# One transposed tile per unit of queries or keys, with the bucket codes compared in PSUM

## The chip, the cores and the metric

The kernel runs on one core of a Trainium2 chip. The metric is the time of one execution on the device, in microseconds. Of the kernel before, three runs are known, with a median of 793.76 us (791.67 to 797.49), and one profiled execution.

## The reference

```python
def _attn_ref(q, k, v, proj):              # q, k, v: 2 x 8 heads x 768 x 64, proj: 64 x 6
    scale = 1.0 / np.sqrt(D)
    q_bits = (np.einsum('bhsd,dk->bhsk', q, proj) > 0).astype(np.int64)
    k_bits = (np.einsum('bhsd,dk->bhsk', k, proj) > 0).astype(np.int64)
    powers = 2 ** np.arange(n_bits)
    q_bucket = np.sum(q_bits * powers, axis=-1)
    k_bucket = np.sum(k_bits * powers, axis=-1)
    mask = q_bucket[:, :, :, None] == k_bucket[:, :, None, :]
    scores = scale * np.matmul(q, k.transpose(0, 1, 3, 2))
    scores = np.where(mask, scores, -1000000000.0)
    ...
    return np.matmul(attn, v)              # attn: softmax of scores

def reference(**kwargs):
    attn_out = _attn_ref(**attn_kwargs)
    x = attn_out.transpose(0, 2, 1, 3).reshape(B * S, H * D)     # 1536 tokens x 512
    x = _moe_ref(x=x, **moe_kwargs)        # x @ w_in, gelu by a sigmoid, @ w_out; 512 -> 2048 -> 512
    return _moe2_ref(x=x, **moe2_kwargs)   # top 2 of 8 experts, 512 -> 1024 -> 512 each
```

Attention is masked by hash buckets: a query sees only keys whose six sign bits under the projection equal its own. A dense layer and a layer of eight experts follow.

## The kernel before

The program has three parts that overlap: 96 attention steps, the dense layer in 6 chunks of 256 tokens, which starts when a chunk's heads are done, and the experts, which start when all tokens are routed. A step g is one block of 128 queries of one head: `qk` on TensorE (scores of 128 x 768 into a PSUM tile `s` of two banks, of which there are two), `rowmax` on VectorE (reads the scores, writes them to SBUF as `e` with their maximum), `expo` on ScalarE, `e_hi` on ScalarE and `e_lo` on VectorE (two float16 halves `er`), a DMA transposition of `er` into `et`, and `pv` on TensorE. In the first 16 steps TensorE transposes `e` instead (`e_turn`).

Queries and keys reach `qk` in units: 24 units of queries (two heads by 256 positions) and 16 units of keys (one head by 768 positions). A number is split into float16 parts, hi and lo. `qk` accumulates two products for a block: slot s=0 of `qt` and `kt` (128 rows: hi and lo parts stacked) and slot s=1 (76 rows: 64 of the hi part and 12 of the bucket code, 65504 or 0 in queries, -65504 or 0 in keys, so that each bit that differs pushes a score far down). For each unit the steps are:

- `load`, `stack_hi` (hi part on VectorE or GpSimd, the remainder on GpSimd), `stack_lo` (lo part on ScalarE), and a DMA transposition of stack `sa` into slot 0 of `qt` or `kt` (L170)
- `buckets`: per block of 128 positions two matmuls with the transposed block as weights and the projection as moving operand (L187, L188), which give 12 columns in the free columns 768 and up of an `s` tile; ScalarE copies them out to `pc` (L192)
- `one_hot`: VectorE compares the two halves of `pc` (L198, two instructions) and writes 0 or 1 into columns 64 to 75 of a second stack `sb`, whose first 64 columns hold the hi part and whose last 52 GpSimd has cleared (L140)
- `stack_end`: ScalarE scales the codes (L205), and a second DMA transposition brings `sb` into slot 1 (L206)

`stack_hi` also writes the hi part a second time, scaled by 1/32 (L150 on ScalarE or L152 on VectorE), since the products of both stacks have to add up in one scale.

All DMAs but the indirect ones are issued from SP's queue, in order. The order of the work comes from numbers in `PARAM`: a unit starts at a step of its own (`KA`, `QA`), `buckets` follow `BK` steps later, `one_hot` `OH` steps later. Up to step 99 a scheduler then sets the order on each engine; from step 100 on it is the order of the code.

Of the kernel before, what the change touches and what calls it, by code (L numbers as in the profile page):

```python
# [8 lines left out]
F32 = mybir.dt.float32  # L9
# [22 lines left out]
NT = S // 128  # L32
# [32 lines left out]

@with_exitstack
def fused(ctx: ExitStack, tc: tile.TileContext, q, k, v, proj, w_in, w_out, w_gate, w_noise, noise,
# [20 lines left out]
    pr = {nm: consts.tile([128, 3, NBITS], F16, name=f"p{nm}") for nm in "qk"}  # L88

    def proj_parts():  # L90
        p32 = rt.tile([128, NBITS], F32, name="p32", tag="zc", bufs=1)
        nc.sync.dma_start(p32[:64], proj)
        nc.sync.dma_start(p32[64:], proj)

# [33 lines left out]

    def stack_hi(nm, b, u):
        x = raw[nm, b, u]  # L130
        nh, n = (2, CT) if nm == "q" else (1, NT)
        if nm == "q":
            sa = att.tile([128, nh, n, 128], F16, name="qsa", bufs=1)
            sb = att.tile([128, nh, n, 128], F16, name="qsb", bufs=2)
        else:

            ks = moe.tile([128, 2, n, 128], F16, name="ks", tag="wraw" if b else "gt", bufs=PARAM["NW"] if b else 4)
            sa, sb = ks[:, 0:1], ks[:, 1:2]
        rows[nm, b, u] = sa, sb
# [7 lines left out]
        yield  # L147
        m, o = PARAM["SC"](nm, b), sa[:, :, :, h0:h0 + 64].rearrange(FL)
        if m == "A":
            nc.scalar.activation(o, hi, AF.Copy, scale=1.0 / SH)  # L150
        else:
            (nc.gpsimd if m == "P" else nc.vector).tensor_scalar(o, hi, 1.0 / SH, 0.0, op0=OP.mult, op1=OP.add)  # L152

    def stack_lo(nm, b, u):
        x = raw.pop((nm, b, u))
        sa, sb = rows[nm, b, u]
        hp, i = u
        h0 = 64 if nm == "q" else 0
        nc.scalar.activation(sa[:, :, :, h0:h0 + 64].rearrange(FL), x.rearrange(FL), AF.Copy, scale=SH)
        if nm == "q":  # L160
            xt = att.tile([128, 2, 2, CT, 128], F16, name="qt", bufs=3)
            qts[b, hp, i] = xt
        elif i == 0:
            xt = att.tile([128, 2, 2, NT, 128], F16, name="kt", bufs=4)
            kts[b, hp] = xt
# [3 lines left out]
        rows[nm, b, u] = sb, dst
        nc.sync.dma_start_transpose(dst[:, 0].rearrange("p h c t -> p (h c) t"), sa.rearrange("p h c d -> p (h c d)"))  # L170

    def buckets(nm, b, u):
        sb, xt = rows[nm, b, u]
        nh, n = (2, CT) if nm == "q" else (1, NT)
        w0 = nh * n * 2 * NBITS
# [3 lines left out]
        a0 = s.get("end", S)
        s["end"] = a0 + w0  # L180
        assert s["end"] <= 1024
        pb = s["ps"][:, a0:a0 + w0].rearrange("p (m k) -> p m k", k=2 * NBITS)
        w = pr[nm].rearrange("p a b -> p (a b)")
# [10 lines left out]
    def one_hot(nm, b, u):  # L194
        pc = bks.pop((nm, b, u))
# [711 lines left out]
    def start(g, f, *a):  # L907
        early.setdefault(g, []).append((f, a))
# [343 lines left out]
```

## Time and profile before

| | |
|---|---|
| median of 3 runs | 793.76 us (791.67 to 797.49) |
| profiled execution | 794.73 us, span 793.0 us |
| TensorE matmul | 703.5 us busy, 89% of the span |
| VectorE, ScalarE, GpSimd | 63%, 58%, 34% of the span |
| DMA queue of SP | 125.04 MB, 68.6% of the time of 16 DMA engines |

The span is what lies between the first and the last instruction of the profiled execution; its own time is 1.7 us longer. Shares of the span are means over stretches with different limits, so the stretches are read one by one. A busy time of TensorE counts instructions in flight and is not its peak rate.

### The profile page before, as it was taken

The page shows a single profiled execution, that of the slowest core. Times are in us where ns is not written, and L with a number is a line of the kernel's source. Part 1 is how long each engine was busy: PE and PEld are TensorE (multiplying, and loading weights), DVE is VectorE, ACT ScalarE, POOL GpSimd, SP SyncE. Part 2 cuts the span into 40 slices and gives each one's busy share as a digit, 9 for nine tenths or more (in the row PEclk, how much of TensorE's full clock was granted, in tenths as well). Part 3 has the DMA queues.
Part 4 walks back from the last instruction along what each step waited for, and adds up shares of the span by engine and source line. Part 5 has one row for each costly group of instructions (what it writes and reads, how often), then busy time and mean ns, then how long its engine had stood idle before and what let it go on. Part 6 is the DMA issues. An engine that isn't in the chain of part 4 may idle for free. (4 is left out here: it accounts for less than half of the span.)

```text
span 793.0 us, 14888 instructions
## 1 busy us (share of the span) xinstructions
PE 703.5 (89%) x5408; PEld 432.5 (55%) x5409; DVE 501.4 (63%) x1251; ACT 457.2 (58%) x974; POOL 265.8 (34%) x338
## 2 busy tenths in 40 slices
PE   1776778998988988889989999999999999999995
PEld 0444446646854665467448667466555545555452
DVE  7986889896876778568568815665744526345220
ACT  4688877766876687468658614445543534435220
POOL 7446455641453345025222223322031120302203
PEclk9976788999999999999999999999999999999998
DMA  8999589999999999995697581568978668484213
GB/s 218 234 277 260 164 193 187 274 260 215 179 200 185 174 187 212 187 186 98 101 182 138 102 286 27 132 245 205 277 120 250 179 133 251 64 266 85 28 17 44
DMA packets 266941, 139.19 MB, mean 176 GB/s; under 512 B 224176, under 2 KB 242672, under 8 KB 266864
## 3 DMA queue, kind: packets, MB, share of 16 engines
q1 hardware_dynamic: 260848, 125.04, 68.6%
q0 software_dynamic: 6016, 13.16, 9.4%
q8 instruction: 43, 0.70, 0.4%
q14 instruction: 34, 0.28, 0.1%
HBM read 61.48 MB, written 23.20 MB: 107 GB/s over the span
## 5 line engine op out<-in xcount | busy, mean ns | idle before, releaser
L468 PE MATMUL h<-xt,wi 128*128 128x256 f16 x1152 | 140.4, 278 | 9.5 <-ACT xt L394 5.6
L846 PE MATMUL ph<-xg,ew 128*128 128x400 f16 (+2 forms) x864 | 132.8, 314 | 1.0 <-DVE ht L857 1.0
L786 DVE SCALAR_TENSOR_TENSOR ew<-w,ew 128x1024 f16<-128x1024 f32 x64 | 77.7, 1225 | 86.3 <-ACT ew L785 86.3
L479 PE MATMUL px<-wo,gt 128*128 128x512 f16 x576 | 131.1, 380 | 0.0
L468 PEld LDWEIGHTS <-wi 128*128 128x128 f16 x1152 | 112.9, 100 | 31.3 <-issue 11.8
L877 PE MATMUL py<-ew,ht 128*128 128x512 f16 x576 | 126.0, 379 | 0.0
L251 PE MATMUL s<-kt,qt 128*128 128x512 f16 (+3 forms) x384 | 90.9, 359 | 36.6 <-DVE e L263 24.1
L894 POOL DMA_INDIRECT out_dram<-yo,ti x32 | 50.0, 1564 | 204.4 <-ACT yo L887 190.2
L846 PEld LDWEIGHTS <-ew 128*128 128x128 f16 x864 | 80.4, 98 | 51.0 <-issue 2.8
L320 DVE SCALAR_TENSOR_TENSOR er<-e,mx,er 128x768 f16<-128x768 f32 x68 | 72.1, 1063 | 43.7 <-ACT er L311 39.9
L877 PEld LDWEIGHTS <-ht 128*128 128x128 f16 x576 | 56.3, 98 | 66.8 <-issue 0.2
L263 DVE TENSOR_SCALAR_CACHE_REDUCE e<-s 128x768 f32<-128x768 f32 x96 | 90.6, 948 | 1.6 <-PE pt L290 0.5
L272 ACT ACTIVATE e<-e,mx 128x768 f32<-128x768 f32 x96 | 89.4, 931 | 1.7
L514 POOL TENSOR_TENSOR gt<-th,gt 128x512 f16<-128x512 f32 x48 | 57.3, 1194 | 98.0 <-ACT gt L512 97.9
L479 PEld LDWEIGHTS <-gt 128*128 128x128 f16 x576 | 55.0, 98 | 63.2 <-issue 1.3
L311 ACT ACTIVATE er<-e,mx 128x768 f16<-128x768 f32 x68 | 62.9, 930 | 33.0 <-DMA et<-er 31.3
L251 PEld LDWEIGHTS <-qt 76*128 76x128 f16 (+1 forms) x384 | 35.9, 103 | 67.5 <-issue 30.2
L887 ACT ACTIVATE yo<-py,wv 128x512 f32<-128x512 f32 x24 | 16.5, 687 | 93.7 <-PE py L877 57.1
L785 ACT ACTIVATE ew<-w 128x1024 f16<-128x1024 f32 x64 | 66.2, 1048 | 0.1
L856 ACT ACTIVATE ht<-ph 128x400 f16<-128x400 f32 (+2 forms) x72 | 33.4, 465 | 53.0 <-PE ph L846 52.5
L365 PE MATMUL pv<-et,vt 128*64 128x256 f16 x720 | 50.7, 283 | 8.7 <-DMA et<-er 8.5
L857 DVE SCALAR_TENSOR_TENSOR ht<-ph,ht 128x400 f16<-128x400 f32 (+2 forms) x72 | 37.5, 523 | 28.0 <-ACT ht L856 27.9
(230 smaller groups left out, 909.5 us busy)
## 6 DMA issues: line engine op xcount, KB each, us to landing
w<-in_moe_w_dram SPq DMA_DIRECT2D x64, 512.0 KB
wraw<-in_moe_w_in_dram SPq DMA_DIRECT2D x16, 512.0 KB
wraw<-in_moe_w_out_dram SPq DMA_DIRECT2D x16, 512.0 KB
slots<-blank SPq DMA_DIRECT2D x6, 1032.0 KB
v<-in_v_dram SPq DMA_DIRECT2D x24, 192.0 KB
out_dram<-zeros SPq DMA_DIRECT2D x13, 256.0 KB
k<-in_k_dram SPq DMA_DIRECT2D x16, 192.0 KB
q<-in_q_dram SPq DMA_DIRECT2D x24, 128.0 KB
```

The source lines that it names most:

```text
L251: nc.tensor.matmul(ps[:, n0 * 128:n1 * 128], qt[:kr, s, h, t, :], kt[:kr, s, h, n0:n1, :].rearrange("p c t -> p (c t)"), start=(s == 0), s ...
L263: nc.vector.tensor_scalar(e32, st[g]["ps"][:, :S], -FAR, -TOP, op0=OP.max, op1=OP.max, accum_out=mx[:, 0:1])
L272: nc.scalar.activation(e32, e32, AF.Exp, scale=0.125, bias=st[g]["mx"][:, 1:2], accum_out=sms[b, cc, hp][:, 2 * h + t:2 * h + t + 1] if g ...
L311: nc.scalar.activation(er[:, 0], st[g]["e"], AF.Copy, scale=r)
L320: nc.vector.scalar_tensor_tensor(er[:, 1], d["e"], d["mx"][:, 3:4], er[:, 0], op0=OP.mult, op1=OP.subtract)
L468: nc.tensor.matmul(ph[:, a, :], wi[ws][:, d, f0:f0 + 128], xt[:, d, xs, :], start=(d == 0 and ws == 0 and xs == 0), stop=(d == HP - 1 and ...
L479: nc.tensor.matmul(px, gts[ci, f // 2][:, gs, f % 2, t * 128:t * 128 + 128], wo[ws][:, f, :], start=(f == 0 and gs == 0 and ws == 0), stop ...
L514: eng.tensor_tensor(gt[:, 1], th, gt[:, 0], op=OP.subtract)
L785: nc.scalar.activation(hi, x, AF.Copy, scale=SW1 if j == 0 else SW2)
L786: nc.vector.scalar_tensor_tensor(lo, x, SW1 if j == 0 else SW2, hi, op0=OP.mult, op1=OP.subtract)
L846: nc.tensor.matmul(ph[:, :c1 - c0], w[:, ws, d * FE + f * 128:d * FE + f * 128 + 128], xg[e, p][:, xs * HP + d, :], start=(d == 0 and ws = ...
L877: nc.tensor.matmul(py, ht[:, f, hs, t * 128:t * 128 + 128], w[:, ws, f * DM:(f + 1) * DM], start=(i == 0), stop=(i == n - 1))
```

## The change

One stack per unit is transposed, not two. Its transposed slot 0 holds the hi and the lo part, and slot 1 takes its first 64 rows from slot 0 by a copy within SBUF (`second`: ScalarE for queries, 64 x 512, and GpSimd for keys, 64 x 768). `buckets` now has the projection (12 columns) as weights and the transposed blocks as moving operand, two blocks or 256 positions at a time, so that codes come out with codes on partitions: 2 groups of 12 partitions for a unit of queries, 3 for a unit of keys, each in a stretch of 32 partitions of its own, three accumulating matmuls per group, in the same free columns of an `s` tile. `codes` compares them where they are, in PSUM, with a threshold per partition, and writes 65504 or -65504 or 0 straight into rows 64 to 75 of slot 1 (12 x 256 per instruction, two instructions for a unit of queries, three for one of keys). The copy to `pc`, `one_hot`, `stack_end`, the scaled second hi part and the clearing of `sb` go away. `BK` goes from 3 to 2. The scale of the scores becomes 32 times as large, which `expo` takes back. Per run the DMA transpositions of queries and keys go from 80 to 40.

```diff
+PARAM.update(NH=lambda nm, b, hp: 2 if nm == "q" else 1, KC=lambda nm, b: "A" if nm == "q" else "D", EM=0, Q3=2, X3=4, QT=3)
+PARAM.update(KC=lambda nm,b:"A" if nm=="q" else "P")
+PARAM.update(BK=2,OH=3)
...
-        nc.gpsimd.memset(sb[:, :, :, KB:].rearrange(FL), 0.0)
-        h0 = 0 if nm == "q" else 64
-        hi = sb[:, :, :, 0:64].rearrange(FL)
+        h0 = 64 if nm == "q" else 0
+        hi = ks[:, :, :, h0:h0 + 64].rearrange(FL)
...
-        m, o = PARAM["SC"](nm, b), sa[:, :, :, h0:h0 + 64].rearrange(FL)
-        if m == "A":
-            nc.scalar.activation(o, hi, AF.Copy, scale=1.0 / SH)
-        else:
-            (nc.gpsimd if m == "P" else nc.vector).tensor_scalar(o, hi, 1.0 / SH, 0.0, op0=OP.mult, op1=OP.add)
...
+    def second(nm, b, u, j, k):
+        xt = rows[nm, b, u][:, :, j:j + k]
+        h0 = 64 if nm == "q" else 0
+        y, x = (xt[a:a + 64, s].rearrange("p h c t -> p (h c t)") for a, s in ((0, 1), (h0, 0)))
+        m = PARAM["KC"](nm, b)
+        if m == "A":
+            nc.scalar.activation(y, x, AF.Copy, scale=SH if nm == "q" else 1.0)
+        elif nm == "q":
+            (nc.gpsimd if m == "P" else nc.vector).tensor_scalar(y, x, SH, 0.0, op0=OP.mult, op1=OP.add)
+        else:
+            (nc.gpsimd if m == "P" else nc.vector).tensor_copy(y, x)
...
-        for h in range(nh):
-            for c in range(n):
-                o = pb[:, h * n + c, :]
-                nc.tensor.matmul(o, xt[:, 0, h, c, :], w[:, :2 * NBITS], start=True, stop=False)
-                nc.tensor.matmul(o[:, NBITS:], xt[:, 0, h, c, :], w[:, 2 * NBITS:], start=False, stop=True)
-
-        pc = att.tile([128, nh * n, 2 * NBITS], F32, name="pc", bufs=PARAM["PC"])
-        bks[nm, b, u] = pc
-        nc.scalar.activation(pc, pb, AF.Copy)
+        for i in range(m):
+            h, c = divmod(2 * i, n)
+            o = 32 * (j0 + i)
+            parts.append((s["ps"][o:o + 2 * NBITS, S:], xt[:, 0, h, c:c + 2].rearrange("p c t -> p (c t)"),
+                          xt[64:KB, 1, h, c:c + 2].rearrange("p c t -> p (c t)"), edge[o:o + 2 * NBITS]))
+        for a in range(3):
+            for o, x, _, _ in parts:
+                nc.tensor.matmul(o, w[:, a], x, start=(a == 0), stop=(a == 2))
+        bks[nm, b, u, j] = parts
...
-            nc.vector.tensor_tensor(oh[:, :, j * NBITS:(j + 1) * NBITS], pc[:, :, :NBITS], pc[:, :, NBITS:],
-                                    op=OP.is_le if j == (nm == "q") else OP.is_gt)
+    def codes(nm, b, u, j):
+        for o, _, y, t in bks.pop((nm, b, u, j)):
+            nc.vector.tensor_scalar(y, o, t, -BIG if nm == "k" else BIG,
+                                    op0=OP.is_le if nm == "k" else OP.is_gt, op1=OP.mult)
             yield
...
-        nc.scalar.activation(oh, oh, AF.Copy, scale=-BIG if nm == "k" else BIG)
-        nc.sync.dma_start_transpose(xt[:, 1].rearrange("p h c t -> p (h c) t"), sb.rearrange("p h c d -> p (h c d)"))
...
-        start(g + PARAM['BK'], buckets, nm, b, u)
-        at(g + oh, one_hot, nm, b, u)
-        soon(g + oh + 1, stack_end, nm, b, u)
+        for i, j in enumerate(range(0, nh, k)):
+            start(g + PARAM['BK'] + i, second, nm, b, u, j, k)
+            start(g + PARAM['BK'] + i, buckets, nm, b, u, j, k)
+            at(g + oh + i, codes, nm, b, u, j)
```

SP's queue of before, in the stretch of steps 31 to 36 of the first batch (`et<-er` is the transposition of a step, `qt<-qsa` the first and `qt<-qsb` the second of a unit of queries, `slots` a plain clearing transfer):

```order
L170 DMA_TRANSPOSE qt_2140<-qsa_2109 128x4x128
L324 DMA_TRANSPOSE et_2091<-er_2047 128x12x128
L324 DMA_TRANSPOSE et_2091<-er_2086 128x12x128
L121 DMA q32_2156<-in_q_dram 128x2x128
L567 DMA slots_121<-blank_106 128x4x1032
L206 DMA_TRANSPOSE qt_2055<-qsb_2030 128x4x128
L324 DMA_TRANSPOSE et_2181<-er_2137 128x12x128
L567 DMA slots_121<-blank_106 128x1032
L581 DMA_TRANSPOSE xrt_2197<-xr_2166 128x8x128
L324 DMA_TRANSPOSE et_2181<-er_2175 128x12x128
L206 DMA_TRANSPOSE qt_2140<-qsb_2110 128x4x128
```

SP's queue of the changed kernel around the same unit of queries, now `qt_2010`:

```order
L178 DMA_TRANSPOSE qt_2010<-qs_1991 128x4x128
L342 DMA_TRANSPOSE et_1974<-er_1969 128x12x128
L588 DMA slots_122<-blank_107 128x4x1032
L342 DMA_TRANSPOSE et_2056<-er_2007 128x12x128
L588 DMA slots_122<-blank_107 128x1032
L602 DMA_TRANSPOSE xrt_2072<-xr_2043 128x8x128
L342 DMA_TRANSPOSE et_2056<-er_2052 128x12x128
L178 DMA_TRANSPOSE qt_2159<-qs_2139 128x4x128
```

The second transposition of each unit is gone, and nothing else has taken its place in the row.

VectorE's queue of before at the end of that unit (L263 is `rowmax`, L198 `one_hot`, which reads the copy `pc`):

```order
L320 SCALAR_TENSOR_TENSOR er_2175<-e32_2169,mx_2168,er_2175 128x768
L502 SCALAR_TENSOR_TENSOR xr_2166<-px_1966,xr_2166 128x512
L502 SCALAR_TENSOR_TENSOR xr_2166<-px_2183,xr_2166 128x512
L198 TENSOR_TENSOR qsb_2110<-pc_2212 128x4x6 x2
L263 TENSOR_SCALAR e32_2288,mx_2287<-s_2199 128x768
```

VectorE's queue of the changed kernel there (L273 is `rowmax`, L215 `codes`):

```order
L160 TENSOR_SCALAR ks_2731<-k32_2561 128x6x64
L273 TENSOR_SCALAR e32_2080,mx_2079<-s_2031 128x768
L215 TENSOR_SCALAR qt_2010<-s_2031,edge_90 12x256 x2
L703 COPY xr_3067<-tok_104 128x2
L337 SCALAR_TENSOR_TENSOR er_2052<-e32_2046,mx_2045,er_2052 128x768
L523 SCALAR_TENSOR_TENSOR xr_2043<-px_1845,xr_2043 128x512
```

The comparison now reads the score tile `s_2031` itself, right behind the `rowmax` of that tile, so the tile is free one or two instructions later than before.

## Rows read from the trace of the kernel before

**Rows 1.** Busy time by stretch: us, PE, PEld, DVE, ACT, POOL, clock, DMA, GB/s.

```profile
0.00:120.00 120.00, 75.41 (x566) 47.78 (x567) 99.36 (x227) 88.72 (x220) 65.34 (x111) 0.84 0.91 223
120.00:415.00 295.00, 262.61 (x2220) 172.02 (x2219) 219.50 (x579) 207.50 (x477) 117.17 (x127) 0.97 0.96 189
415.00:793.00 378.00, 365.49 (x2625) 212.73 (x2625) 182.53 (x447) 160.95 (x277) 83.27 (x100) 0.99 0.61 150
```

**Rows 2.** Chain in order of time, two pieces of the experts: start, us, what.

```profile
549.19 1.42 PE py L871 x48
...
552.76 16.26 PE ph L846 x96
```

**Rows 3.** Groups by line, 120 to 415 us: busy, mean ns, idle before, releasers.

```profile
L251 PE MATMUL s<-kt,qt 76*128 76x512 f16 (+3 forms) x256 | 55.2, 334 | 16.4 <-DVE e L263 9.7 <-DMA qt<-qsb 6.6
...
L365 PE MATMUL pv<-et,vt 128*64 128x256 f16 x565 | 40.6, 285 | 7.4 <-DMA et<-er 7.2
...
L187 PE MATMUL s<-pq,qt 128*128 128x12 f16 x64 | 5.2, 170 | 5.2 <-DMA qt<-qsa 5.2
...
L187 PE MATMUL s<-pk,kt 128*128 128x12 f16 x48 | 3.4, 168 | 0.5 <-DMA kt<-ks 0.5
```

**Rows 4.** The same view, 0 to 120 us.

```profile
L251 PE MATMUL s<-kt,qt 128*128 128x512 f16 (+1 forms) x96 | 29.3, 435 | 20.2 <-DVE e L263 14.4 <-DMA qt<-qsb 5.1 <-ACT pc L192 0.6
...
L187 PE MATMUL s<-pk,kt 128*128 128x12 f16 x48 | 3.8, 179 | 14.2 <-DMA kt<-ks 13.6 <-ACT wi L447 0.6
```

**Rows 5.** DMA queue, 265 to 295 us: packets, MB, share of 16 engines.

```profile
q1 hardware_dynamic: 18052, 5.18, 99.3%
```

**Rows 6.** DMA queue, 460 to 480 us, mostly plain loads of weights.

```profile
q1 hardware_dynamic: 3626, 4.68, 78.7%
```

**Rows 7.** SP's timeline from 200 us: start, us, instruction.

```profile
201.48 1.62 SPq L170 DMA_TRANSPOSE kt<-ks  x1
203.19 1.45 SPq L324 DMA_TRANSPOSE et<-er  x1
```

**Rows 8.** Line 206, 120 to 415 us: ns min/median/max, first and last start.

```profile
L206 SPq DMA_TRANSPOSE qt<-qsb x17: 1189/1500/1934, 120.6 to 412.0; - x17
L206 SPq DMA_TRANSPOSE kt<-ks x8: 1210/1525/1581, 217.4 to 283.6; - x8
```

**Rows 9.** TensorE's timeline, first and last matmul of the first unit of keys.

```profile
13.61 0.19 PE L187 MATMUL s<-pk,kt 128*128 128x12 f16 x1 [13.61 <-DMA kt<-ks]
...
13.92 0.17 PE L188 MATMUL s<-pk,kt 128*128 128x6 f16 x1
```

**Rows 10.** Line 152: ns min/median/max, first and last start, form.

```profile
L152 DVE TENSOR_SCALAR ks<-ks x16: 243/480/1262, 4.3 to 267.8; 128x384 f16<-128x384 f16 x16
L152 DVE TENSOR_SCALAR qsa<-qsb x12: 211/416/970, 4.4 to 187.7; 128x256 f16<-128x256 f16 x12
```

**Rows 11.** Groups by line, whole span, work that the change takes away.

```profile
L198 DVE TENSOR_TENSOR qsb<-pc 128x24 f16<-128x24 f32 x48 | 10.6, 260 | 0.2 <-ACT pc L192 0.2
...
L192 ACT ACTIVATE pc<-s 128x48 f32<-128x48 f32 (+1 forms) x40 | 8.0, 206 | 2.1 <-PE s L188 2.1
...
L198 DVE TENSOR_TENSOR ks<-pc 128x36 f16<-128x36 f32 x32 | 6.7, 248 | 1.7 <-ACT pc L192 1.5
...
L205 ACT ACTIVATE qsb<-qsb 128x48 f16<-128x48 f16 x24 | 5.7, 237 | 8.4 <-DVE qsb L198 8.2
...
L150 ACT ACTIVATE qsa<-qsb 128x256 f16<-128x256 f16 x12 | 4.9, 409 | 5.0 <-DMA qt<-qsa 3.5 <-POOL qsb L144 1.3
```

**Rows 12.** The same view, nearest rows for the price of added work.

```profile
L447 ACT ACTIVATE wo<-wraw 128x512 f16<-128x512 f32 x16 | 10.6, 661 | 0.8 <-POOL wraw L444 0.8
...
L144 POOL TENSOR_SCALAR qsb<-q 128x256 f16<-128x256 f32 x12 | 13.0, 1087 | 14.7 <-DMA q<-in_q_dram 14.2
...
L444 POOL TENSOR_SCALAR wraw<-wraw 128x512 f32<-128x512 f32 x8 | 5.4, 679 | 6.1 <-DVE wraw L431 4.6 <-issue 1.4
...
L381 DVE TENSOR_TENSOR xn<-pv,xn 128x256 f32<-128x256 f32 x7 | 2.9, 413 | 0.0
```

More of the change, by code (lines that the diff above doesn't have):

```diff
@@ L87, in fused @@
     nc.vector.tensor_copy(ident32, ident)
-    pr = {nm: consts.tile([128, 3, NBITS], F16, name=f"p{nm}") for nm in "qk"}
+    pr = {nm: consts.tile([128, 3, 2, NBITS], F16, name=f"p{nm}") for nm in "qk"}
+    edge = consts.tile([128, 1], F32)
     def proj_parts():
@@ L93, in proj_parts @@
         nc.sync.dma_start(p32[64:], proj)
+        lane = rt.tile([128, 2], I32, name="lane", tag="zt", bufs=1)
+        nc.gpsimd.iota(lane[:, 0:1], pattern=[[0, 1]], base=0, channel_multiplier=1)
+        nc.vector.tensor_scalar(lane[:, 1:2], lane[:, 0:1], 31, 0, op0=OP.bitwise_and, op1=OP.bitwise_or)
+        nc.vector.tensor_scalar(edge, lane[:, 1:2], NBITS, -(2.0 ** -100), op0=OP.is_ge, op1=OP.mult)
         p3 = rt.tile([128, 3, NBITS], F16, name="p3", tag="z", bufs=1)
@@ L157, in stack_lo @@
         hp, i = u
-        h0 = 64 if nm == "q" else 0
[L159 to L165, printed above, removed]
-        else:
-            xt = kts[b, hp]
-        dst = xt if nm == "q" else xt[:, :, i:i + 1]
@@ L169, in stack_lo @@
[L169 to L175, printed above, removed]
+        nh, n = heads(nm, b, hp), CT if nm == "q" else NT
+        h0 = 0 if nm == "q" else 64
+        nc.scalar.activation(ks[:, :, :, h0:h0 + 64].rearrange(FL), x.rearrange(FL), AF.Copy, scale=SH)
@@ new lines, in stack_lo @@
+        if nm == "q":
+            dst = qts[b, hp, i] = att.tile([128, 2, nh, n, 128], F16, name="qt", bufs=PARAM["QT"])
+        else:
+            if i == 0:
+                kts[b, hp] = att.tile([128, 2, 2, n, 128], F16, name="kt", bufs=4)
+            dst = kts[b, hp][:, :, i:i + nh]
+        rows[nm, b, u] = dst
+        nc.sync.dma_start_transpose(dst[:, 0].rearrange("p h c t -> p (h c) t"), ks.rearrange("p h c d -> p (h c d)"))
+    def second(nm, b, u, j, k):
+        xt = rows[nm, b, u][:, :, j:j + k]
+        h0 = 64 if nm == "q" else 0
+        y, x = (xt[a:a + 64, s].rearrange("p h c t -> p (h c t)") for a, s in ((0, 1), (h0, 0)))
[4 more added lines that the diff above has]
+            (nc.gpsimd if m == "P" else nc.vector).tensor_scalar(y, x, SH, 0.0, op0=OP.mult, op1=OP.add)
+        else:
+            (nc.gpsimd if m == "P" else nc.vector).tensor_copy(y, x)
@@ L176, in buckets @@
+    def buckets(nm, b, u, j, k):
+        xt = rows[nm, b, u][:, :, j:j + k]
+        n = CT if nm == "q" else NT
+        m = k * n // 2
         s = st.get(now[0] + 2)
-        if s is None:
+        if s is None or s.get("used", 0) + m > 4:
             s = {"ps": pss.tile([128, 1024], F32, name="s")}
[L179 to L183, printed above, removed]
@@ L214, in v_load32 @@
         vfs[cc, hp] = x
-        for h in range(2):
-            PARAM['LE'](nc).dma_start(x[:, h].rearrange("p c d -> p (c d)"), v[0, 2 * hp + h].rearrange(
-                "(p c) d -> p (c d)", c=NT))
+        PARAM['LE'](nc).dma_start(x.rearrange("p h c d -> p h (c d)"),
+                                  v[0, 2 * hp:2 * hp + 2].rearrange("h (p c) d -> p h (c d)", c=NT))
     def v_hi(b, u):
@@ L304, in e_hi @@
             return
-        er = att.tile([128, 2, S], F16, name="er")
+        if PARAM["EM"]:
+            if g % 2 == 0:
+                st["er"] = att.tile([128, 2, NT, 2, 128], F16, name="er")
+            er = st["er"][:, :, :, g % 2]
+            st[g]["e3"] = st[g]["e"].rearrange("p (c k) -> p c k", c=NT)
+        else:
+            er = att.tile([128, 2, S], F16, name="er")
+            st[g]["e3"] = st[g]["e"]
         st[g]["er"] = er
@@ L946, in stacks @@
         soon(g + 1, stack_lo, nm, b, u)
-        start(g + PARAM['BK'], buckets, nm, b, u)
-        at(g + oh, one_hot, nm, b, u)
-        soon(g + oh + 1, stack_end, nm, b, u)
+        nh = heads(nm, b, u[0])
+        k = 2 if nm == "q" else 1
+        for i, j in enumerate(range(0, nh, k)):
+            start(g + PARAM['BK'] + i, second, nm, b, u, j, k)
+            start(g + PARAM['BK'] + i, buckets, nm, b, u, j, k)
+            at(g + oh + i, codes, nm, b, u, j)
     for b in range(B):
@@ L953, in fused @@
             g = b * NCH * 16 + 4 * hp
+            for h in range(0, 2, heads("k", b, hp)):
+                stacks(PARAM["KA"].get((b, hp, h), g - LK + 2 * h), "k", b, (hp, h))
             for h in range(2):
-                stacks(PARAM["KA"].get((b, hp, h), g - LK + 2 * h), "k", b, (hp, h))
                 gv = next(x for x in range(g, NU, 16) if x >= FU) - PARAM["VA"].get((b, hp, h), LV - h)
-                at(gv - 3, load, "v", b, (hp, h))
+                if h % heads("v", b, hp) == 0:
+                    at(gv - 3, load, "v", b, (hp, h))
                 soon(gv, v_hi, b, (hp, h))
```

69 lines of the change are left out of this document (36 added, 33 removed).

## The prediction

> **What bounds the kernel now.** I read the windows by stretch first [rows 1]. From 415 us on TensorE is busy 365.5 of 378 us, and the chain there is one row of matmuls behind another [rows 2]: the change touches one unit of queries in that stretch, so it stays as it is, and whatever is saved ahead of it moves the end by the same amount. Between 120 and 415 us TensorE is busy 262.6 of 295 us, 32.4 us idle, while the DMA engines are busy 96% of the time, 283 us. No other engine is near its limit (VectorE 74%, ScalarE 70%). In the front, 0 to 120 us, TensorE idles 44.6 us, VectorE is busy 83%, ScalarE 74% and DMA 91%: a mixed bound.
>
> Then the groups of TensorE, to see whom it waits for [rows 3, 4]. In the middle 19.5 us of its idle time end on transpositions: 6.6 on `qt<-qsb`, the second one of queries, which the change removes, and 5.2 + 0.5 + 7.2 on the first ones of queries and keys and on `et`. Another 9.7 us end on `rowmax` (VectorE), which frees a score tile. In the front 13.6 us are the first load and transposition, which stay, 5.1 us are `qsb` and 14.4 us `rowmax`. Last SP's queue: there a transposition takes about 1.5 us to issue, and the next stands right behind it [rows 7, 8].
>
> **The change part by part.**
>
> Transpositions. Between 265 and 295 us, 5.18 MB took 99.3% of 30 us, nearly all of it transpositions: 29.8 / 5.18 = 5.75 us per MB on all 16 engines [rows 5]. A unit of keys is 128 x 768 x 2 bytes, 0.197 MB or 1.13 us; one of queries 0.131 MB or 0.75 us. Over the span 16 x 1.13 + 24 x 0.75 = 36 us of DMA time go. By line 206, 17 + 8 of them start in the middle [rows 8]: 12.8 + 9.0 = 21.8 us, and 25 x 1.5 = 37.5 us of SP's queue. 8 + 6 lie in the front: 13.5 us. Of the 21.8 us only what TensorE waits for can come back. The 6.6 us on `qsb` go outright. The other 12.9 us of waits on transpositions shrink, since queue and engines are freer: at least nothing, at most all of it. I take two thirds, 8.6, because the queue gets back more time (37.5 us) than the engines (21.8 us), and both exceed the 12.9 us. Middle: **-15 us**, bounds -6.6 and -21.8.
>
> Trainium skill, "Advanced Engine Details and Errata", section X-Bar Transpose (TRN2): transpose DMAs are as fast as regular ones. The trace differs: plain loads of weights moved 4.68 MB in 15.7 us, 3.4 us per MB [rows 6], against 5.75. By the page's rule the 3.8 MB removed in the middle would be worth 12.9 us, not 21.8, and the larger end of the middle would shrink to that.
>
> Front. The 5.1 us on `qsb` go: the first product with slot 1 needs one transposition, not two in a row. Work on VectorE there changes little (next part), so I take **-4 us**. If the lighter DMA queue also brings weights earlier it could be -12; if VectorE, 83% busy, takes it all back, +3.
>
> VectorE. `one_hot` goes, 10.6 + 6.7 = 17.3 us [rows 11], and so do the 28 scaled copies, 16 x 0.48 + 12 x 0.42 = 12.7 us by their medians [rows 10]: 30 us. `codes` adds 24 x 2 + 16 x 3 = 96 instructions of 12 x 256 from PSUM. Nearest is L381, 128 x 256 out of PSUM, 0.413 us [rows 12]; time goes by columns, so 96 x 0.41 = 39 us. Net +9 us, over 415 us of which VectorE is idle 96. It isn't free where it stands: right behind `rowmax`, on the tile that TensorE waits for. A unit holds its tile 2 or 3 x 0.41 = 0.8 to 1.2 us longer. TensorE's waits on `rowmax` in the middle are 9.7 us in 64 steps, 0.15 us a step, and only 25 steps carry codes: I take **+2 us**, with ends 0 and 25 units x 1 us = 25.
>
> TensorE. The 12 matmuls of a unit of keys stand 13.92 - 13.61 = 0.31 us apart from first to last [rows 9], and the 8 of a unit of queries by the same spacing 0.2: 16 x 0.31 + 24 x 0.2 = 10 us. The new ones: in L871 four groups of 32 columns of weights run at once, 48 matmuls of 256 columns in 1.42 us, 0.118 us for a round of four [rows 2]. A unit has three rounds, 0.36 us, 40 units 14 us. If groups didn't overlap, 288 x 0.118 = 34 us. I take the first, as it is the same form of output: **+3 us** where TensorE is near its bound; other end +24, of which the middle would carry some 16.
>
> ScalarE. L192 8.0 us, L150 4.9 and L205 5.7 (queries alone) go [rows 11]; 24 copies of 64 x 512 come, like L447, 0.66 us each [rows 12]: 15.9. It comes out lighter. The copy waits for a landed transposition with `expo` and `e_hi` queued behind it, but on ScalarE's queue it stands a step or more behind the `stack_lo` that feeds the transposition. Cost nothing; cover: ScalarE's 30% idle time in the middle.
>
> GpSimd. 40 clearings go, 16 copies of 64 x 768 come. L444 does 512 columns in 0.68 us, L144 256 columns in 1.09 [rows 12]: between 1.0 and 3.3 us a copy, 16 to 52 us. I take 1.0, since a plain copy is nearer to L444. GpSimd is busy 40% in the middle and 54% in the front, which hides it; else see the third rival.
>
> `BK` of 2 lets TensorE ask for the transposed unit a step earlier. In the order of the queues, past the first units, several transpositions of `et` stand between a unit's transposition and its bucket; cost nothing, with those waits as cover, and 5.2 us again if they aren't enough [rows 3].
>
> Sum: -15 - 4 + 2 + 3 = -14 us against the profiled execution of 794.7: 780.7. That execution lies 1.0 us over the median, so I predict **780 us**.
>
> **The rivals.**
>
> 1. The whole DMA time comes back. If the middle goes as fast as its DMA engines allow, -21.8, and the front gains 12: 794.7 - 34 + 5 = 766, less 1: 765. For it: DMA 96% busy, SP back to back. Against: TensorE has 32.4 us idle there, 9.7 of them not on DMA.
>
> 2. No difference. The pace of the middle is set by the circle `rowmax`, `expo`, `e_hi`, `e_lo`, so that a lighter DMA only waits longer. Then the waits on `qsb` alone go, 6.6 + 5.1 = 11.7, and the added 2 + 3 and the longer hold of tiles (4) come back: 794.7 - 11.7 + 5 + 4 - 1 = 791. For it: VectorE's and ScalarE's queues wait on one another. Against: rows 3 name transpositions for twice as much as VectorE.
>
> 3. GpSimd's copies cost their 3.3 us. Eight stand in the first third of the front on a queue that the remainders of queries and keys share, 26 us in all, and the keys of the first heads come late; front +10 in place of -4, middle as forecast: 780 + 14 = 794. The scaled copies on VectorE, 243 ns at best, took 480 in the median and up to 1262 [rows 10], so something held VectorE up for the length of whole instructions. Trainium skill, "SBUF — State Buffer", section Who interferes with whom: GpSimd and VectorE's fast copy modes share a port pair, and one blocks the other for the whole instruction. The rows agree with that, and no row shows this copy.
>
> 4. Slower. Tiles held by `codes` become the bound: there are two score tiles, `codes` free one only after `rowmax`, and if VectorE runs late, 24 x 0.8 + 16 x 1.2 = 38 us are exposed. With -4 - 15 + 3 from the rest it is 794.7 + 22, less 1: 816 at the worst, with two thirds exposed 803. It decides as soon as TensorE's waits on VectorE, 24 us now [rows 3, 4], grow by more than 16 us. Against it: VectorE is idle 25% of the middle.
>
> 5. The columns don't overlap: +16 on the middle, 780 + 16 = 796.
>
> **How the numbers follow.** Forecast 0.45 (770 to 787), rival 1 0.18, rival 2 0.15, rival 3 0.07, rival 4 0.10, rival 5 0.05. Within 1% of 793.8 is 785.8 to 801.7, about what a measurement of this kernel tells from no change. Faster: the forecast but for its upper end, and rival 1: 0.62. Same: that end, rivals 2, 3 and 5 and the milder half of 4: 0.29. Slower: 0.09. The range takes in rival 1 to just under its value and rival 2, 3 and 5: 764 to 799.
>
> **What the profile after would show.** The line of `qt<-qsb` gone from TensorE's releasers and its share of `et` and first transpositions under 8 us in the middle; DMA packets fewer by 24,576 x 256 bytes, 6.3 MB; `codes` near 0.41 us; the six matmuls of a unit of queries in about 0.36 us; `second` at 0.66 us on ScalarE and 1 us on GpSimd; from the first expert to the end the same length as now. Wrong would be: TensorE's waits on `rowmax` or `codes` above 40 us, copies on GpSimd near 3 us, or a middle that is as long as before with the DMA engines at 90%.

## The result, and the profile after

| | before | after |
|---|---|---|
| median | 794.82 us (791.67 to 797.49) | 806.01 us (804.05 to 806.43) |
| profiled execution | 794.73 us, span 793.0 | 806.43 us, span 804.8 |
| VectorE busy | 501.4 us | 532.0 us |
| DMA queue of SP | 125.04 MB, 68.6% | 118.75 MB, 61.2% |

Medians are of four runs each. The ratio after to before is 1.0138, 95% interval 1.0094 to 1.0181: the change costs 11 us (8 to 14), where 14 us less were predicted. The granted clock of TensorE is not the reason: its mean over the profiled execution is 0.962 before and 0.966 after, and in none of the three stretches below is it lower than in [rows 1].

First the windows by stretch, for comparison with [rows 1] (columns as there; the last stretch is longer because the span is).

```profile
0.00:120.00 120.00, 72.74 (x459) 39.82 (x461) 101.58 (x214) 84.98 (x190) 62.07 (x101) 0.85 0.71 190
120.00:415.00 295.00, 265.47 (x2189) 170.13 (x2188) 243.00 (x576) 207.76 (x432) 120.70 (x114) 0.98 0.85 179
415.00:805.00 390.00, 374.16 (x2668) 217.26 (x2665) 187.37 (x456) 166.01 (x286) 83.36 (x100) 0.99 0.61 147
```

The DMA engines were relieved as intended, 96% to 85% in the middle and 91% to 71% in the front. But VectorE went from 219.5 to 243.0 us in the middle and TensorE is no less occupied than before. Next the score matmuls by line (ns min/median/max, first and last start), before and then after.

```profile
L251 PE MATMUL s<-kt,qt x384: 270/379/634, 15.6 to 446.6; 128*128 128x512 f16 x96, 76*128 76x512 f16 x96
```

```profile
L261 PE MATMUL s<-kt,qt x384: 270/377/634, 20.0 to 458.0; 128*128 128x512 f16 x96, 76*128 76x512 f16 x96
```

The first score starts 4.4 us later and the last 11.4 us later; from there to the end of the span it is 346.4 us before and 346.8 after. So all of the loss lies ahead of the last score, and the tail is unchanged, as predicted. Now TensorE's groups in the middle, against [rows 3], and in the front, against [rows 4].

```profile
L261 PE MATMUL s<-kt,qt 128*128 128x512 f16 x252 | 52.5, 329 | 8.2 <-DVE e L273 4.7 <-DVE qt L215 2.9 <-DVE kt L215 0.4
L386 PE MATMUL pv<-et,vt 128*64 128x256 f16 x576 | 41.4, 285 | 11.1 <-DMA et<-er 9.8 <-DVE cum L726 1.3
L210 PE MATMUL s<-qt,pq 128*12 128x256 f16 x96 | 7.5, 273 | 1.7 <-DVE e L273 0.9 <-DMA qt<-qs 0.8
L210 PE MATMUL s<-kt,pk 128*12 128x256 f16 x72 | 4.3, 290 | 0.0
```

```profile
L261 PE MATMUL s<-kt,qt 128*128 128x512 f16 (+1 forms) x92 | 23.9, 393 | 20.4 <-DVE kt L215 9.7 <-DVE qt L215 5.6 <-DVE e L273 5.1
...
L210 PE MATMUL s<-kt,pk 128*12 128x256 f16 x72 | 5.8, 356 | 15.0 <-DMA kt<-ks 13.7 <-DVE qt L215 1.3
L210 PE MATMUL s<-qt,pq 128*12 128x256 f16 x42 | 4.6, 342 | 7.0 <-DMA qt<-qs 6.0 <-DVE e L273 1.0
```

`qt<-qsb` is gone from the list (6.6 and 5.1 us before). In the front the wait has only changed its name: 20.2 us before, 20.4 now, 15.3 of it on `codes`. In the middle the wait on `et` did not shrink with the freer queue but grew from 7.2 to 9.8 us: the releaser (what ended the wait) that the row names is a DMA, yet in the program its transposition can start only when VectorE has written `er`. Last, the new instructions and the queue.

```profile
L215 DVE TENSOR_SCALAR kt<-s,edge x48: 469/478/483, 12.9 to 291.6; 12x256 f16<-12x256 f32 x48
L215 DVE TENSOR_SCALAR qt<-s,edge x48: 474/478/493, 15.8 to 435.2; 12x256 f16<-12x256 f32 x48
...
who waited for it (us, times):
  PE s L261: 19.3, 15
```

```profile
DMA packets 241020, 132.88 MB, mean 165 GB/s; under 512 B 198256, under 2 KB 216752, under 8 KB 240944
...
q1 hardware_dynamic: 234928, 118.75, 61.2%
```

The queue carries 6.3 MB less, as forecast.

Where does the lag arise? By the starts of `rowmax` in the two timelines, the changed kernel is 0.9 us ahead at step 33 (176 us), 5.0 us behind at step 39, 15.7 at step 57, 7.6 at step 75 and 12.3 at step 93. The 40 us from 200 on lie in the stretch of the loss, in which the units of keys of the second batch follow one another (windows as above, after and then before).

```profile
200.00:220.00 20.00, 14.48 (x139) 10.70 (x138) 18.02 (x37) 14.73 (x35) 14.84 (x14) 1.00 0.87 174
220.00:240.00 20.00, 18.69 (x142) 11.37 (x142) 19.67 (x57) 14.21 (x32) 12.75 (x14) 0.91 0.81 197
```

```profile
200.00:220.00 20.00, 19.90 (x224) 16.52 (x223) 18.00 (x53) 16.09 (x41) 9.05 (x10) 1.00 0.96 188
220.00:240.00 20.00, 17.38 (x133) 9.61 (x132) 14.89 (x54) 15.69 (x40) 12.89 (x15) 0.91 1.08 198
```

VectorE is busy 37.7 of 40 us there, against 32.9, and TensorE 33.2 against 37.3. VectorE's timeline in it shows what fills it (start, us, instruction), and GpSimd's what ran beside it.

```profile
229.03 1.47 DVE L215 TENSOR_SCALAR kt<-s,edge 12x256 f16<-12x256 f32 x3
230.53 1.76 DVE L160 TENSOR_SCALAR ks<-k 128x384 f16<-128x384 f32 x1
...
233.38 1.83 DVE L724 TENSOR_TENSOR xr<-xr,d 128x2 f32<-128x2 f32 x1
```

```profile
230.92 1.15 POOL L535 TENSOR_TENSOR gt<-th,gt 128x512 f16<-128x512 f32 x1
...
234.05 1.15 POOL L535 TENSOR_TENSOR gt<-th,gt 128x512 f16<-128x512 f32 x1
```

Codes take 1.47 us in a row. Beside them stand instructions that last longer than usual: L160 takes 0.40 us in the median, and L724, on two columns, 0.16. Both end just behind an instruction of GpSimd: L160 at 232.29, 0.22 us after it, and L724 at 235.21, 0.01 us after it.

Over the whole span VectorE's busy time rose by 30.6 us, where the lengths of the instructions that came and went give 14 (`codes` 45.8, against 17.3 for `one_hot` and 14.3 for the scaled copies). Others became longer, the rounding of keys (L160) by 3.6 us in all, and fewer run into one another: busy time counts overlapping instructions once, and the lengths exceed it by 63 us before and by 55 after.

### The profile page after: what moved, and what is told of

Same layout as the page of the kernel before. It is cut to its first block, busy times and chain, and to the rows that moved or that the text cites. A ratio compares the mean times of both kernels' runs of the same rounds, so it can differ in the third digit from the quotient of the medians.

```text
span 804.8 us, 14500 instructions
## 1 busy us (share of the span) xinstructions
PE 712.4 (89%) x5312; PEld 427.2 (53%) x5313; DVE 532.0 (66%) x1245; ACT 458.7 (57%) x906; POOL 266.1 (33%) x315
## 3 DMA queue, kind: packets, MB, share of 16 engines
q1 hardware_dynamic: 234928, 118.75, 61.2%
## 5 line engine op out<-in xcount | busy, mean ns | idle before, releaser
L261 PE MATMUL s<-kt,qt 128*128 128x512 f16 (+3 forms) x384 | 84.4, 344 | 31.6 <-DVE e L273 12.2
L273 DVE TENSOR_SCALAR_CACHE_REDUCE e<-s 128x768 f32<-128x768 f32 x96 | 90.8, 948 | 8.4 <-PE pt L300 5.0
L386 PE MATMUL pv<-et,vt 128*64 128x256 f16 x720 | 50.8, 284 | 11.3 <-DMA et<-er 10.0
```

What stands on the lines that cost most here:

```text
L261: nc.tensor.matmul(ps[:, n0 * 128:n1 * 128], qt[:kr, s, h, t, :], kt[:kr, s, h, n0:n1, :].rearrange("p c t -> p (c t)"), start=(s == 0), s ...
L273: nc.vector.tensor_scalar(e32, st[g]["ps"][:, :S], -FAR, -TOP, op0=OP.max, op1=OP.max, accum_out=mx[:, 0:1])
```

## Experiments

Times are given against the kernel before, which ran on the same chip each time, as ratios; 0.1% is 0.8 us. An interval is some 0.4% to either side, so a difference of two kernels is known to about 4 us.

**Doubling each part.** Four runs put a price on the parts of the change by adding to the changed kernel.

`BK` undone:

```diff
-PARAM.update(BK=2,OH=3)
+PARAM.update(BK=3,OH=3)
```

> Changed kernel with BK back at 3 instead of 2, nothing else: bucket matmuls and the second copies stand one step later, in the step of their codes. Theory 1 (VectorE and TensorE pay: the 96 codes stand between rowmax and the next score matmul, and the bucket matmuls take 20.7 us of TensorE against 12.1 before): placement matters little, 800 to 810 us. Theory 2 (asking for the transposed unit a step earlier is what costs, TensorE then stands in its queue before a unit that has not landed): 795 or less, and TensorE's waits on the first transpositions in front (13.7 us on keys) shrink by more than 5 us.

1.0129 (1.0063 to 1.0194): the same as the change. The first score then starts at 15.7 us, as in the kernel before, and still the median hardly moves. `BK` is not the cause. The waits do change. TensorE's score matmuls waited 19.3 us for `codes` in the changed kernel, and here (us, times):

```profile
  PE s L261: 0.8, 2
```

and TensorE's wait on the transposed keys falls from 13.7 to 2.9 us. In their place stand `rowmax`, 23.1 us against 12.2 (0 to 450 us), and 11.3 us for another instruction of VectorE (L446). The time is the same.

Codes twice:

```diff
+            for _ in range(2):
-            nc.vector.tensor_scalar(y, o, t, ...)
+                nc.vector.tensor_scalar(y, o, t, ...)
```

> Changed kernel with every comparison of codes done twice (96 more VectorE instructions of 0.478 us, 45.9 us). Theory 1 (time on VectorE between rowmax and the release of the score tile is on the path): +20 to +45 us over the changed kernel, 826 to 850. Rival (VectorE has room, idle a third of the time, and the loss is elsewhere): +0 to +10, 806 to 816.

1.0597 (1.0566 to 1.0627), 36.5 us over the changed kernel for 45.9 us of work: each us of it costs 0.80, the slope in what follows. (The score tile is held longer too; e7 adds work without that.) The score matmuls of this run, as above:

```profile
L262 PE MATMUL s<-kt,qt x384: 270/379/634, 29.7 to 497.2; 128*128 128x512 f16 x96, 76*128 76x512 f16 x96
```

Bucket matmuls twice:

```diff
-        for a in range(3):
+        for a in (0, 1, 2, 0, 1, 2):
```

> Changed kernel with the bucket matmuls of every unit done twice (288 more of TensorE's, 40 units x 0.22 to 0.33 us at full clock and up to 0.6 us in the stretches at half clock: 13 to 16 us). Theory 1 (TensorE's time before the last score step counts fully): +10 to +16 us, 816 to 822. Rival (TensorE waits anyway, its idle time takes it in): +0 to +4, 806 to 810.

1.0245 (1.0208 to 1.0281), 8.5 us over the changed kernel. A second set occupies TensorE for 0.32 us a unit more (in the timelines the next matmul starts 0.75 us behind the first of a unit, against 0.43), 12.8 us in 40 units at full clock: a slope of about two thirds.

Transpositions put back, into a tile that nobody reads:

```diff
         nc.sync.dma_start_transpose(dst[:, 0].rearrange(...), ks.rearrange("p h c d -> p (h c d)"))
+        idle = att.tile([128, NT, 128], F16, name="idle", bufs=1)
+        nc.sync.dma_start_transpose(idle[:, :nh * n], ks.rearrange("p h c d -> p (h c d)"))
```

> Changed kernel with 40 transpositions put back on SP's queue, one behind each unit's, into a tile that nobody reads (6.3 MB, 36 us of the DMA engines). It tells what the relief of the DMA was worth. Theory 1 (the relief was worth little, since TensorE's waits moved to codes and rowmax): +0 to +5 us, 806 to 811. Rival (the relief did give 10 to 20 us and the new work took more than that): +10 to +20 us, 816 to 826.

1.0340 (1.0308 to 1.0372), 16 us over the changed kernel. The queue's 125.04 MB are back, and the last score is at 476.3 us. So the relief was real and worth nearly what had been forecast (19 us); the new work took more than that. Nobody waits for these transpositions, so 16 us is the price of queue and engines alone, without the wait on `qsb` itself.

```profile
L263 PE MATMUL s<-kt,qt x384: 270/379/634, 20.8 to 476.3; 128*128 128x512 f16 x96, 76*128 76x512 f16 x96
```

In such runs the mean granted clock falls as well, from 0.966 to 0.951 (e2), 0.952 (e4) and 0.947 (e7, below), and the same 5312 matmuls keep TensorE busy for 726.1 us in e2 in place of 712.4. The slopes contain this.

**The hold of the tile, or VectorE's time?** In the next run ScalarE copies a unit's buckets out of the score tile, so that VectorE no longer holds it.

```diff
+        pc = att.tile([128, 256], BF16, name="pc", bufs=3)
+        nc.scalar.activation(pc[o0:o1], s["ps"][o0:o1, S:], AF.Copy)
...
-        bks[nm, b, u, j] = parts
+        bks[nm, b, u, j] = [(pc[32 * (j0 + i):32 * (j0 + i) + 2 * NBITS], None, y, t)
+                            for i, (_, _, y, t) in enumerate(parts)]
```

> Changed kernel, but ScalarE copies a unit's buckets out of the score tile in one instruction (as bfloat16; the weights are padded with zeros to 32 columns so that all rows are written) and VectorE compares from that copy: the score tile is released by ScalarE, as in the kernel before, and the comparison reads the main on-chip memory in place of PSUM. Adds 40 copies on ScalarE. Theory 1a (what hurts is the hold of the score tile, TensorE waits 19.3 us on codes): those waits vanish and the time falls by 10 to 25 us, to 781 to 796. Theory 1b (what hurts is VectorE's time itself): if an instruction stays near 0.48 us, 800 to 806; if it gets cheaper, 0.84 of what VectorE saves (the slope of the doubled codes, 38.7 of 45.9 us) comes back.

1.0251 (1.0219 to 1.0283), 9 us slower than the change. TensorE's waits, 0 to 450 us (us in total, times, longest):

```profile
PE s L268 <- DVE e L280: 25.1, 18, 5.7
PE s L213 <- DMA kt<-ks: 15.8, 4, 11.4
```

The waits on codes are gone, and those on `rowmax` went from 12.2 to 25.1 us. Theory 1a, by which 10 to 25 us come back, falls as it was put. But the run also added 14.5 us of copies on ScalarE, ahead of `expo`, whose price is not known, so a smaller part of the hold may be hidden behind them. VectorE saved nothing, by a surprise:

```profile
L222 DVE TENSOR_SCALAR kt<-pc,edge x48: 272/278/1598, 13.8 to 297.5; 12x256 f16<-12x256 bf16 x48
L222 DVE TENSOR_SCALAR qt<-pc,edge x48: 268/278/1746, 17.4 to 444.9; 12x256 f16<-12x256 bf16 x48
```

0.28 us in the median, but 0.48 in the mean, as in PSUM: some instructions took six times their length. Two of one unit, and what GpSimd did:

```profile
302.78 1.03 DVE L222 TENSOR_SCALAR qt<-pc,edge 12x256 f16<-12x256 bf16 x1
...
304.07 0.28 DVE L222 TENSOR_SCALAR qt<-pc,edge 12x256 f16<-12x256 bf16 x1
```

```profile
302.59 1.15 POOL L542 TENSOR_TENSOR gt<-th,gt 128x512 f16<-128x512 f32 x1 [0.18 <-ACT gt L540]
```

The first ends at 303.81, 0.07 us behind GpSimd's instruction; during the second GpSimd is idle. The two other long ones that the timeline lists by themselves, at 89.87 and 143.03 us, end 0.09 and 0.08 us behind one.

The same comparison on GpSimd (`nc.vector` to `nc.gpsimd` in that line):

> As the run before, but GpSimd compares from the copy: VectorE loses all 45.8 us of codes, GpSimd, idle two thirds of the time, gains 96 instructions. Theory 1b (VectorE's time is on the path with a slope of 0.84): 806 - 38 = 768 and at most 785, TensorE's waits on VectorE halved. Rival (GpSimd is late with the codes, or holds VectorE up, so that only the wait changes its name): 795 or more, with waits of TensorE on codes written by GpSimd.

1.0637 (1.0599 to 1.0675), 40 us slower than the change. One comparison takes 1.13 us there (median); GpSimd is busy 386.7 us in place of 266.1, and in the front 90 of 120 us, while VectorE, at 60 us, waits. The rival holds: codes and remainders come late.

```profile
L222 POOL TENSOR_SCALAR qt<-pc,edge x48: 1134/1140/1925, 18.5 to 476.0; 12x256 f16<-12x256 bf16 x48
```

Idle work on VectorE behind the last code of a unit, in a scratch tile:

```diff
+        for _ in range(2 if nm == "q" else 3):
+            spare = att.tile([12, 3, 128], F32, name="spare", bufs=1)
+            nc.vector.tensor_scalar(spare, ident32[:12, None, :].to_broadcast([12, 3, 128]), edge[:12], BIG,
+                                    op0=OP.is_gt, op1=OP.mult)
```

> Changed kernel with 96 more VectorE instructions on a scratch tile of 12 rows, behind the last code of each unit: they take VectorE's time without holding a score tile longer. Theory 1b (VectorE's time itself): +0.84 us for each us they are busy, as with the doubled codes. Theory 1a (the hold): less than a third of that, 806 to 818.

1.0552 (1.0505 to 1.0599), 33 us over the changed kernel for 96 x 0.595 = 57 us of work that holds no tile. The row shows that it wasn't where it had been written: nothing depends on it, and it was drawn into the first 209 us. Even so, more than half of it is paid, although it holds no tile: VectorE's time costs by itself. VectorE's busy time rose by 40.6 us only, in e2 by 43.6; per us of busy time the two runs pay 0.81 and 0.84.

```profile
L220 DVE TENSOR_SCALAR spare<-ident,edge x96: 570/595/602, 3.6 to 208.5; 12x384 f32<-12x384 f32 x96
```

The rounding of keys moved from VectorE to GpSimd (`HE=lambda nm,b:'DPPP'[2*(nm=='k')+b]`):

> Changed kernel with the upper halves of the keys rounded on GpSimd in place of VectorE (16 instructions of 0.70 us, 11.1 us off VectorE, at the end of which the same GpSimd takes the remainder). Theory 1b: 0.84 of 11.1 us, so 806 - 9 = 797. Rival (these 16 instructions stand where VectorE has room, or GpSimd delays the keys): 803 to 812.

1.0349 (1.0311 to 1.0388), 17 us slower than the change, against both expectations. An instruction of 0.40 us on VectorE (median) takes 1.50 on GpSimd, in whose queue the remainder and the copy of `second` stand behind it, and TensorE's wait on the transposed keys went from 13.7 to 27.4 us:

```profile
L160 POOL TENSOR_SCALAR ks<-k x16: 1497/1498/2302, 3.5 to 250.1; 128x384 f16<-128x384 f32 x16
```

**The copies into slot 1.** ScalarE waits 12.2 us for landed transpositions in `second`, with `expo` and `e_hi` behind it, a wait that I had put at nothing. Three runs issue it two steps later:

```diff
-            start(g + PARAM['BK'] + i, second, nm, b, u, j, k)
+            soon(g + 4 + i, second, nm, b, u, j, k)
```

> Changed kernel with the copies into slot 1 (second) issued two steps later and behind expo and e_hi of their step, not ahead of them; the buckets stay where they are. Theory 2a (ScalarE's queue is on the path: it waits 12.2 us for landed transpositions in second with expo and e_hi behind it, and GpSimd 11.2 us with the remainders behind it; run e5 put 14.5 us on ScalarE and lost 11.6): those waits go and 8 to 12 us come back, 794 to 798. Rival (the waits would stand elsewhere anyway): 802 to 808.

1.0129 (1.0090 to 1.0169), the same as the change. But the wait didn't go either; ScalarE still waited in this line:

```profile
  DMA qt<-qs: 14.3, 13
```

So this run doesn't tell whether the wait costs; it stays open.

With the copies of queries on VectorE as well (`KC` "D" for queries):

> As the run before, and the copies of queries on VectorE in place of ScalarE: 24 x 0.63 us off ScalarE, 24 copies of 64 x 512 half-precision values within the main on-chip memory onto VectorE, which by its scaled copies before (243 ns at best, 0.48 in the median) should take 0.25 to 0.5 us, 6 to 12 us. With slopes of about 0.8 for both engines: 2 to 7 us faster than the run before. Rival (VectorE is nearer to its limit than ScalarE): as fast or slower by up to 5.

1.0263 (1.0220 to 1.0305), 11 us over the run before. The 24 copies take 10.7 us on VectorE, which now has the wait for them too, 15.8 us, with `rowmax` behind it. VectorE's busy time rises by 14.1 us (532.2 to 546.3), which at 0.8 would be the 11 us; whether the work or the moved wait costs, the run doesn't tell.

With `BK` 3:

> As e9, and BK back at 3. Theory 2a: as e9 within 3 us. Rival (BK and second hurt together: TensorE asks for a unit early and everything behind it waits): 5 us or more faster than e9.

1.0151 (1.0111 to 1.0191): as e9.

**Two units in one step.** `buckets` takes a new score tile when a step's units need more than the four groups of rows (32 partitions each) that one tile has: steps 1, 37, 47 and 51, the last three in the stretch of the loss.

```diff
+PARAM["QA"].update({(0, 0, 2): 2, (1, 0, 0): 38, (1, 0, 2): 48})
+PARAM["KA"].update({(1, 2, 1): 50})
```

> Changed kernel with four units moved by one step, so that no two units whose buckets need more than four row groups together fall on one step (queries of 1, 37 and 47 to 2, 38 and 48, keys of 51 to 50). Theory 3 (such a pair takes a third score tile out of the two, and TensorE waits for rowmax and codes twice): the jump between steps 40 and 56 shrinks by 8 us or more, 790 to 798. Rival (it is VectorE's load in that stretch, which stays): 802 to 808.

> The run before with BK back at 3. Theory 3: within 4 us of the run before, 788 to 800. Rival: 802 to 808.

1.0189 (1.0159 to 1.0220) and 1.0111 (1.0073 to 1.0150): no gain. And the kernel before with the same own tiles:

```diff
-        if s is None:
+        if s is None or (s.get("end", S) > S and now[0] < 60):
             s = {"ps": pss.tile([128, 1024], F32, name="s")}
```

> The kernel before, where the second unit that falls on a step takes a score tile of its own (steps 1, 37, 47 and 51), as it does in the changed kernel; nothing else is changed. Theory 3: 6 to 14 us slower than the kernel before, 801 to 809, between steps 40 and 56. Rival: within 3 us of it.

0.9948 (0.9922 to 0.9973), 4 us *faster* than the kernel before. Theory 3 falls. This is the only version here that beats both kernels; why it does is not known.

**What VectorE's time costs in the kernel before.**

```diff
-        for j in range(2):
+        for j in (0, 1, 0, 1, 0, 1):
             nc.vector.tensor_tensor(oh[:, :, j * NBITS:(j + 1) * NBITS], ...
```

> The kernel before with each comparison of one_hot done three times: 160 more VectorE instructions, twice 17.3 us, 34.6 us. If VectorE's time costs as much in the kernel before as in the changed one (0.84): +29 us, 823. If the DMA covers it there: +0 to +12, 794 to 806, and then the removal of 31 us from VectorE gave little back, which is a part of what is missing.

1.0172 (1.0133 to 1.0211), 13.7 us for 54.6 - 17.3 = 37.3 us (`one_hot` takes 31.8 + 22.8 us here): a slope of 0.37, not 0.80. Work of this kind was cheap where it stood. (VectorE's busy time rose by 28.9 us only; per us of it, 0.47.)

**One half at a time.** The other half is written as in the kernel before, with two transpositions, a copy of the buckets on ScalarE, and codes on tokens:

```diff
...
+        if nm in OLD:
+            start(g + PARAM['BK'], buckets_old, nm, b, u)
+            at(g + oh, one_hot, nm, b, u)
+            soon(g + oh + 1, stack_end, nm, b, u)
+            return
...
```

> The change for keys alone (BK 3): keys as in the changed kernel, queries with two transpositions and codes on tokens, as in the kernel before (their codes compared with zero and scaled in one instruction). DMA relief 16 x 1.13 = 18 of 36 us, half of the 18.4 us that the idle transpositions cost: -9. VectorE +22.9 for codes, -14.4 for the work removed; TensorE +3.1. Additive account (0.84 on what comes, 0.34 on what goes): -9 + 19 - 5 + 2 = +7, 803. Theory 4 (VectorE is dear only once both halves load it; up to there it costs 0.34): -9 + 3 + 2 = -4, 792.

> The change for queries alone (BK 3): keys with two transpositions and codes on tokens. DMA relief 24 x 0.75 = 18 us, worth 9. VectorE +22.9 for codes, -10.6 for one_hot and -5 for the copies; TensorE +5.5. Additive account: -9 + 19 - 5 + 3 = +8, 804. Theory 4: -9 + 2.5 + 3 = -4, 792.

> Neither half of the change: queries and keys both with two transpositions, in the way the unchanged half was written in the two runs before (BK 3). If the halves themselves cost: within 4 us of the kernel before, 793 to 801. If the way of writing costs: 803 or more, and the two runs before are read against this one, by which the keys alone would be 813 less it and the queries alone 807 less it.

Keys alone 1.0214 (1.0165 to 1.0263), queries alone 1.0135 (1.0092 to 1.0177), neither 1.0090 (1.0054 to 1.0125). The last is a control, 7 us over the kernel before. The old half as written here has three small matmuls for a block where the kernel before has two (TensorE is busy 711.3 us against 703.5), and the control keeps the small edits of the change besides, such as one transfer in place of two for the first values (`v_load32`), which no run prices; which of these costs the 7 us was not tried. Against the control the keys cost 10 us and the queries 3.5, which is within the error. Neither half gains; theory 4, by which the first half would, falls. The whole with `BK` 3 (e1) is only 3 us over this control, so the halves don't add up. VectorE's busy time doesn't either: over the 502.2 us of e18 it rises by 20.7 us with the keys, by 17.8 with the queries and by 27.4 with both (e1). That fits, but it is not shown to be the reason. The middle of e18 and of e16 (columns as above) shows the trade that the keys make, DMA 0.96 to 0.89 for 19 us of VectorE:

```profile
120.00:420.00 300.00, 266.83 (x2360) 177.24 (x2359) 219.85 (x579) 204.02 (x455) 119.54 (x127) 0.97 0.96 187
```

```profile
120.00:420.00 300.00, 264.26 (x2238) 173.42 (x2237) 238.68 (x578) 203.77 (x444) 127.31 (x132) 0.96 0.89 181
```

## Why the prediction was wrong

Put together from the runs, the change is: -16 us for the transpositions (e4); +36 for the codes, 45.8 us at 0.80 (e2); -11 for the 30 us taken off VectorE, at 0.37 (e15); +5 for TensorE, 7.4 us at two thirds (e3). That is +14, and +11 was measured. The prices are those of more or less work of a kind at one place, and they need not add up exactly; that the scaled copies, 12.7 of the 30 us, give back 0.37 like `one_hot` was not tried.

- **VectorE: the step that failed.** The prediction said "Net +9 us, over 415 us of which VectorE is idle 96", priced only the hold of the tile, and took +2 with ends 0 and 25. By the prices of the runs it is 36 - 11 = +25, the upper end. Two things were off. An idle share is not cover: 96 us idle in 415 hide nothing in stretches where VectorE is 90 and 98% busy, like the two from 200 us. And the net of +9 was too small: VectorE's busy time rose by 30.6 us. The instruction was a sixth dearer, 0.478 us against 0.41, and the rest is overlap and longer neighbours, which a sum of lengths leaves out. How the +25 comes about can be told in two ways that these runs don't separate: `codes` at 0.80 came and work worth 0.37 went, or 30.6 us of busy time came at the 0.81 to 0.84 of e7 and e2, which is about 25 too.
- **Transpositions: nearly right in size.** -15 and -4 stand against 16 us. But the sum of waits that were named (19.5 us in the middle, so that the larger bound of -21.8 went beyond what it was taken from) was no promise: `qsb` went, and waits on `codes` and `et` took its place. The sign of under 8 us on `et` and first transpositions in the middle didn't come: it is 9.8 + 0.8. The 5.75 us per MB were also read less cleanly than "nearly all of it transpositions" says: 754 of the 18052 packets there are larger ones of plain loads, 0.75 of the 5.18 MB if the others are of 256 bytes.
- **TensorE: mis-sized.** +3 was forecast, from 0.36 us a unit. The groups do run at once, but three rounds at that pace are not the whole: a unit occupies TensorE until the next matmul starts, 0.43 us behind its first (timeline of the change):

```profile
130.57 0.50 PE L210 MATMUL s<-qt,pq 128*12 128x256 f16 x6
131.00 1.26 PE L489 MATMUL h<-xt,wi 128*128 128x256 f16 x10
```

  40 x 0.43 = 17.2 us against the 9.8 us of before.
- **ScalarE and GpSimd.** The lengths were right, 0.63 and 0.82 us against 0.66 and 1.0, so the third rival's 3.3 us didn't come. "Cost nothing" for the wait in `second` was wrong as a description, 12.2 us; its price is open (e9).
- **`BK`: right**, nothing in the time (e1), though the waits change places.
- **The rivals.** The fourth gave 803 to 816 and the time lies there, but not for its reason. It was to decide when TensorE's waits on VectorE grow by more than 16 us; they grew from 24.1 us [rows 3, 4] to 34.7 (`rowmax` 12.2 + 1.9, `codes` 19.3 + 1.3, ahead of 450 us), in e1 the waits on `codes` went without a gain, e5 took the hold away and lost 9 us, and e7 paid for work that holds no tile. So VectorE's time costs without the tile; that the hold adds nothing is not shown. That 803, with two thirds exposed, is so near is luck.
- **The middle** is no shorter than before (the last score lags by 11.4 us, the first by 4.4), with the DMA engines at 85%: the sign set for "wrong" came, nearly as it had been put.

That VectorE's time is dear in the changed kernel is shown (e2, e7), and so is what the transpositions gave back (e4). Why it is dearer than in the kernel before (0.47 per us of busy time in e15), by its place in the queue or because the DMA no longer covers it, is open: e16 to e18 don't decide it.

## What to carry to other kernels

When a change trades one resource for another, price both by the stretch in which they are fullest, and don't take removed work to give back what added work of its length costs: ask of each what stands behind it in its queue, and what it overlaps with. The cheapest way to get those rates is to do the new work twice, and to leave the old work in place without a reader. A wait that disappears from the list tells little as long as the next engine in the chain has not been shown to have room: in e1 19 us of waits on `codes` went, and the time stayed.

## What was not expected of the hardware

- A 12 x 256 comparison takes VectorE 469 to 493 ns from PSUM. From a copy in main on-chip memory it takes 268 ns at best, but up to 1746, and 0.48 us in the mean. The Trainium skill, "SBUF — State Buffer", section Who interferes with whom, says that VectorE's two-port modes share a port pair with GpSimd, and that one blocks the other for a whole instruction. The timeline of e5 agrees with that: the long comparison at 302.78 us ends 0.07 us behind GpSimd's instruction, and the next of its unit, with GpSimd idle, takes 0.28 us. A run with GpSimd kept idle was not made.
- 24 copies moved from ScalarE (15.1 us there) to VectorE (10.7 us) cost 11 us (e10 against e9), although VectorE is idle a third of the span.
- GpSimd is a poor refuge: the moved comparisons took 1.13 us against VectorE's 0.28 from the same copy (e6 and e5, medians), the moved roundings 1.50 against 0.40 (e8), and its queue delayed others.
